# Batch 1's first half as the second chunk, its attention in float32 products, and the check for the general path inside the last feed forward

## Chip, cores and metric

The kernel runs on one core of a Trainium2 chip. The metric is the device time of one execution in microseconds (us), the median of three runs.

## What is computed

Sliding-window attention with a few always visible first keys ("sinks"), followed by a feed forward with a squared ReLU. Everything is float32; 4 batches, 8 heads of 64, 768 positions, model width 512, inner width 2048.

```python
B, H, S, D = 4, 8, 768, 64          # n_sink = 4, window = 128
scores = matmul(q, k.T) / sqrt(D)
keep = (pos[None, :] < n_sink) | ((rel >= 0) & (rel < window))
a = softmax(where(keep, scores, -1e9))
x = matmul(a, v)                     # heads side by side: (B*S, 512)
h = x @ w_in                         # (3072, 2048)
r = maximum(h, 0.0)
g = s * (r * r) + b
out = g @ w_out                      # (3072, 512)
```

## The kernel before

The 3072 tokens are cut into 8 chunks of 384: chunk `c` is half `c % 2` of batch `c // 2`. A first half needs only its own 384 keys; a second half also the block ahead of it and the sinks.

Chunk 0's attention stands alone at the start (`first_slots`), in plain float32 products: a score product `fa` (a float32 product is recorded as two matmuls), a masked minimum on VectorE (L445), an exponential on ScalarE (L449), the division by the row's sum on VectorE (`fn`, L457 to L460), the transpose `fb` (L468, copied out by L472), and the product with v, `fc` (L480), whose result each head copies out by itself into the pair's half of `k.x` (L482, L483). A head is three units of 128 rows.

All later chunks use `attn_slots`: each operand is split into a high part and a rest in a reduced format that TensorE takes as one product (the dtype fp32r of the rows), so that a product is two or three cheaper ones. The splitting is done by ScalarE, VectorE and GpSimd (`prep_head`, L268 to L278; the transposed weights L321 and L322), the sinks of a second half go through a product of their own (L305, L367 to L382).

The feed forward of a chunk is `moe_steps`: for each of 16 blocks `f` of the inner width, `l1(f)` makes 12 matmuls (L521), then L524, L525, L527 and L528 make the two parts of `g`; `l2(f)`, two steps later, makes 9 matmuls (L539). That is 32 steps. While the feed forward of chunk c runs, the slots of the attention of chunk c+1 are dealt out between its steps.

During chunk 0's attention and its feed forward the weights are made from the raw 64-bit words (`make_weight`): per block two ScalarE passes (L198, L199), two VectorE passes (L200, L201), a GpSimd addition (L203), a ScalarE copy (L208) and a subtraction (L214) on VectorE or, for each fourth block, GpSimd. From the second feed forward on they stay in memory.

The order of instructions on each engine is set by a scheduler when the program is built, from the order of the code and from when buffers come free; on the chip each engine takes its instructions in that order. All loads and stores are issued from SyncE's queue (SP).

At the end `bad` collects whether the inputs are outside what this path handles (more sinks or a wider window than laid out for, or a row with nothing to keep); a product `cnt` sums it up, `flag` is loaded into a register of each engine by `values_load`, and `tc.If(go > 0)` runs the general path, which these inputs do not need. The last chunk's three output tiles `ot` use the two buffers of the tag `hl`.

Of the kernel before, what the change touches and what calls it, by code (L numbers as in the profile page):

```python
# [15 lines left out]
P = 128  # L16
B, H, S, D = 4, 8, 768, 64
NS = 16
# [15 lines left out]
E0, LB0, LC0 = 8, 4, 6  # L34
LB, LC, LD, L2 = 2, 4, 1, 2
# [3 lines left out]
def tile_kernel(ctx, tc, qT, kT, k0, v, vsk, n_sink, window, w, s, b, out):  # L39
# [15 lines left out]
    m_all = first.tile([P, 6 * P], MDT, tag="m", name="m_all")  # L55
# [34 lines left out]
    nc.sync.dma_start(lim[:, 0, :], n_sink.partition_broadcast(P))  # L90
    nc.sync.dma_start(lim[:, 1, :], window.partition_broadcast(P))
# [324 lines left out]
    def first_slots():  # L416
        k = Chunk()

        q = [wk.tile([P, NCC, CH], F32, tag=f"x{i}", name=f"q0{i}") for i in range(2)]
        k.x = [wk.tile([P, NCC, CH], F32R, tag=f"x{i}", name=f"x{i}_0") for i in range(2)]  # L420
        kk = first.tile([P, NCC, CH], F32, tag="k0", name="k0")
        vv = first.tile([P, NCC, CH], F32, tag="v0", name="v0")
        cc, tt, zz, sms = {}, {}, {}, {}

        def load():
            nc.gpsimd.memset(q[0][D:], 0.0)
            nc.vector.memset(q[1][:D], 0.0)
            for ps_ in (slice(0, 1), slice(1, NCC)):
                for hh in range(2):
                    hs = slice(hh * D, (hh + 1) * D)  # L430
                    nc.sync.dma_start(q[hh][hs, ps_, :], qT[0, ps_, hs, :CH].rearrange("r e s -> e r s"))
                    if hh == 0:
                        nc.sync.dma_start(kk[:, ps_, :], k0[:, ps_, :])
                nc.sync.dma_start(vv[:, ps_, :].rearrange("p r (n e) -> p r n e", n=BLK),
                                  v[0, ps_, :, :BLK].rearrange("r p n h d -> p r n (h d)"))

        def fa(h, i):
            pr = h // 2
            n = (i + 1) * P
            u = h * BLK + i  # L440
            uu = slice(u, u + 1)
            sc = psO.tile([P, 512], F32, tag="po", name="sc0")
            nc.tensor.matmul(sc[:, :n], q[h % 2][:, pr, i * P:(i + 1) * P], kk[:, pr, :n], start=True, stop=True)
            sm = first.tile([P, CH], F32, name="sm0", tag="sm0", bufs=E0)
            nc.vector.tensor_tensor_reduce(out=sm[:, :n], in0=sc[:, :n], in1=m_full[i], scale=-0.125, scalar=BIG,  # L445
                                           op0=ALU.add, op1=ALU.min, accum_out=negm[:, uu])
            if i == 0:
                zz[h] = first.tile([P, 2, BLK], F32, name="z0", tag="z0", bufs=4)
# [296 lines left out]
```

## Time and profile before

| | us |
|---|---|
| median of 3 runs (from 781.71 to 782.03) | 781.77 |
| the profiled execution, its own time | 781.77 |
| its span, first to last instruction | 780.0 |
| of it TensorE busy | 735.3 |
| VectorE, ScalarE, GpSimd busy | 513.6, 495.5, 268.8 |

The profile is one execution. "Busy" of an engine is the time in which at least one of its instructions was under way; an average over the span hides that the stages have different limits, so that busy times are read by stage below. The profiled execution's own time is that of the median, so that a difference in the span can be set against the median directly.

### The profile page before, as it was taken

Reading aid. Unit: us, or ns where it says so; the run is one execution under the profiler, and the core shown is the slowest. Engines: PE = TensorE matmul, PEld = TensorE weight load, DVE = VectorE, ACT = ScalarE, POOL = GpSimd, SP = SyncE. Lnnn points to the kernel's source line nnn. Section 1 sums busy time; section 2 is a strip of 40 time slices with the busy share of each in tenths; the row PEclk is TensorE's granted clock in tenths of the full one; section 3 lists DMA queues with packets and bytes.
Section 4 is the critical chain, followed back from the end, with each engine's and each line's share of the span. In section 5 each row is a group of like instructions: output and inputs, shape, how many; then the busy total and the mean of one; then the engine's idle time right before and its main releaser. Section 6 shows DMA issues by size and latency. Waiting matters only on the chain.

```text
span 780.0 us, 12112 instructions
## 1 busy us (share of the span) xinstructions
PE 735.3 (94%) x4036; PEld 656.9 (84%) x4036; DVE 513.6 (66%) x1250; ACT 495.5 (64%) x1231; POOL 268.8 (34%) x411
## 2 busy tenths in 40 slices
PE   7977988699999999999999999999999999999996
PEld 4655776579999999899999999899989999899985
DVE  6879998985676467655676466665676466663231
ACT  4886977766666576656666576656666576643222
POOL 3057668652343233322243233332343233210000
PEclk9989999999999999999999999999999999999998
DMA  7636205212112212112112212112111212001001
GB/s 271 273 103 229 105 14 170 76 34 77 42 54 59 73 43 67 35 43 76 43 53 57 76 43 62 40 43 76 43 53 55 77 43 60 21 1 42 1 1 45
DMA packets 28118, 54.21 MB, mean 70 GB/s; under 512 B 3600, under 2 KB 16528, under 8 KB 26128
## 3 DMA queue, kind: packets, MB, share of 16 engines
q1 hardware_dynamic: 28048, 53.36, 21.3%
q8 instruction: 34, 0.56, 0.3%
q14 instruction: 36, 0.29, 0.1%
HBM read 47.06 MB, written 6.29 MB: 68 GB/s over the span
## 4 chain that ended last, share of the span: by engine, by line
PE 76%; DVE 8%; ACT 7%; issue 3%; POOL 3%; DMA 2%; SPq 1%; ACTq 0%; POOLq 0%; DVEq 0%
PE h L521 30%; PE po L539 30%; PE o L354 5%; PE sc L294 2%; PE sc L293 2%; PE tp L317 2%; PE tp L316 2%; ACT w L199 1%; DVE r L525 1%; DMA w<-in_w 1%; PE o L480 1%; POOL w L203 1%; DVE w L201 1%; DVE qs L272 1%; ACT sm L304 1%
## 5 line engine op out<-in xcount | busy, mean ns | idle before, releaser
L521 PE MATMUL h<-x,w 128*128 128x384 f32 x1536 | 299.5, 343 | 8.7 <-DVE hl L322 3.8
L539 PE MATMUL po<-w,g 128*128 128x512 f32 x1152 | 301.6, 403 | 5.7 <-ACT g L527 3.7
L521 PEld LDWEIGHTS h<-x,w 128*128 128x128 f32 x1536 | 269.7, 190 | 14.5 <-issue 4.0
L539 PEld LDWEIGHTS po<-w,g 128*128 128x128 f32 x1152 | 211.6, 191 | 47.7 <-ACT g L527 4.9
L524 ACT ACTIVATE r<-h 128x384 f32<-128x384 f32 x128 | 62.9, 491 | 103.9 <-PE h L521 96.9
L298 DVE CUSTOM_DVE_ANT_0 sm<-sc,msk 128x272 f32<-128x272 f32 (+1 forms) x168 | 70.2, 418 | 78.4 <-PE sc L294 55.9
L525 DVE SCALAR_TENSOR_TENSOR r<-r,sb 128x384 f32<-128x384 f32 x128 | 84.1, 657 | 54.1 <-ACT r L524 54.0
L528 DVE SCALAR_TENSOR_TENSOR g<-r,sb,g 128x384 fp32r<-128x384 f32 x128 | 85.5, 668 | 45.6 <-ACT g L527 43.5
L305 POOL COPY psk<-sm 128x48 f32<-128x48 f32 x168 | 52.2, 311 | 162.9 <-ACT sm L304 161.7
L304 ACT ACTIVATE sm<-sm,negm 128x272 f32<-128x272 f32 (+1 forms) x168 | 85.4, 508 | 23.3 <-DVE negm L298 22.3
L527 ACT ACTIVATE g<-r,sb 128x384 fp32r<-128x384 f32 x128 | 78.7, 614 | 33.2 <-DVE r L525 32.1
L273 POOL TENSOR_TENSOR kl<-kraw,kh 128x544 fp32r<-128x544 f32 (+1 forms) x56 | 74.9, 1337 | 56.8 <-ACT kh L271 55.5
L321 ACT CAST hl<-tp 128x256 fp32r<-128x256 f32 (+1 forms) x168 | 58.8, 352 | 26.4 <-PE tp L317 26.2
L354 PE MATMUL o<-hl,vv 128*128 128x256 f32 (+1 forms) x400 | 71.4, 295 | 1.1 <-DVE hl L322 0.8
L322 DVE TENSOR_TENSOR hl<-tp,hl 128x256 fp32r<-128x256 f32 (+1 forms) x168 | 66.8, 398 | 7.5 <-ACT hl L321 6.7
L278 POOL TENSOR_TENSOR vv<-vraw,vv 128x256 fp32r<-128x256 f32 (+1 forms) x56 | 41.9, 747 | 60.9 <-ACT vv L277 59.0
L354 PEld LDWEIGHTS o<-hl,vv 128*128 128x128 f32 x400 | 54.9, 190 | 2.7 <-DVE hl L322 1.1
L293 PE MATMUL sc<-kh,qs 128*128 128x272 f32 (+1 forms) x168 | 47.8, 284 | 5.8 <-DVE hl L322 4.7
L363 DVE TENSOR_TENSOR xm<-o,y 64x384 f32<-64x384 f32 x56 | 31.0, 553 | 31.5 <-ACT y L362 31.3
L294 PE MATMUL sc<-kl,qs 128*128 128x272 f32 (+1 forms) x168 | 48.5, 289 | 0.0
L203 POOL TENSOR_TENSOR w<-w 128x1024 int32<-128x1024 int32 (+1 forms) x17 | 32.6, 1921 | 42.4 <-DVE z L458 19.3
L317 PE MATMUL tp<-identr,sm 128*128 128x128 f32 x168 | 45.7, 272 | 0.0
(112 smaller groups left out, 852.0 us busy)
## 6 DMA issues: line engine op xcount, KB each, us to landing
w<-in_w SPq DMA_DIRECT2D x15, 1024.0 KB, 8.9
kraw<-in_kT SPq DMA_DIRECT2D x32, 272.0 KB, 2.7
out<-ot SPq DMA_DIRECT2D x24, 256.0 KB, 2.0
qraw<-in_qT SPq DMA_DIRECT2D x28, 192.0 KB, 2.4
kraw<-in_kT SPq DMA_DIRECT2D x24, 208.0 KB, 2.4
vraw<-in_v SPq DMA_DIRECT2D x16, 256.0 KB, 2.7
vraw<-in_v SPq DMA_DIRECT2D x12, 192.0 KB, 2.3
vsraw<-in_vsk SPq DMA_DIRECT2D x28, 64.0 KB, 1.8
```

The source lines that it names most:

```text
L273: nc.gpsimd.tensor_tensor(out=hd.kl[:, :kw], in0=hd.k[:, :kw], in1=hd.kh[:, :kw].bitcast(F32), op=ALU.subtract)
L293: nc.tensor.matmul(sc[:, :n], hd.qs[:, qs], hd.kh[:, c0:c0 + n], start=True, stop=False)
L294: nc.tensor.matmul(sc[:, :n], hd.qs[:, qs], hd.kl[:, c0:c0 + n], start=False, stop=True)
L298: nc.vector.tensor_tensor_reduce(out=sm[:, :n], in0=sc[:, :n], in1=m, scale=-0.125, scalar=BIG, op0=ALU.add, op1=ALU.min, accum_out=negm[: ...
L304: nc.scalar.activation(sm[:, :n], sm[:, :n], AF.Exp, bias=negm[:, uu], scale=-1.0, accum_out=pp.zz[:, i, hh:hh + 1])
L322: nc.vector.tensor_tensor(out=lo, in0=tp[:, a:z], in1=hi.bitcast(F32), op=ALU.subtract)
L354: nc.tensor.matmul(hd.o[:, q0:q0 + n * P], hd.vv[:, kb, :], hd.hl[:, t, c0 * P:(c0 + n) * P], start=(hd.n == 0), stop=(i == BLK - 1 and kb ...
L521: nc.tensor.matmul(h[:, :CH], weight[f][:, 0, wi, cc * P:(cc + 1) * P], x[xi][:, cc, :], start=(i == 0), stop=(i == 11))
L525: nc.vector.scalar_tensor_tensor(out=r, in0=r, scalar=s_ap, in1=r, op0=ALU.mult, op1=ALU.mult)
L527: nc.scalar.activation(gg[:, 0, :], r, AF.Identity, bias=b_ap, scale=1.0)
L528: nc.vector.scalar_tensor_tensor(out=gg[:, 1, :], in0=r, scalar=b_ap, in1=gg[:, 0, :].bitcast(F32), op0=ALU.add, op1=ALU.subtract)
L539: nc.tensor.matmul(po[tb], gg[:, gi, tsl], weight[f][:, 1, wi, :], start=(f == 0 and i == 0), stop=(f == NF - 1 and i == 2))
```

## The change

1. The chunks are worked in the order 0, 2, 1, 3, 4, 5, 6, 7 (`ORDER`). Chunk 2, the first half of batch 1, is now the one whose attention runs beside chunk 0's feed forward, and it is computed by `plain_slots`, the former `first_slots` made to serve both chunks: float32 products, no splitting. Its zero-padded q and v come in per pair of heads (`load_pair`), its tiles share tags with the split path.
2. In `plain_slots`, for both chunks, v is laid out per head with zeros in the other head's 64 columns, so that both heads of a pair add up in one bank of the accumulation memory. One copy (L525) and one subtraction (L526) of 128 partitions per pair take the place of two each of 64 partitions. For v there are 8 loads in chunk 0 instead of 2, in runs of 256 bytes instead of 1536.
3. `out_of_range`, the check, stands after the ninth step of the last feed forward instead of behind everything.
4. The limits and the first pair's v are loaded from ScalarE's queue, the masks `m_all` live on in another pool, and the last chunk's third output tile uses the tag `ot`.

```diff
+ORDER = 0, 2, 1, 3, 4, 5, 6, 7
...
-    nc.sync.dma_start(lim[:, 0, :], n_sink.partition_broadcast(P))
-    nc.sync.dma_start(lim[:, 1, :], window.partition_broadcast(P))
+    nc.scalar.dma_start(lim[:, 0, :], n_sink.partition_broadcast(P))
+    nc.scalar.dma_start(lim[:, 1, :], window.partition_broadcast(P))
...
+                for pr in range(rs.start, rs.stop):
+                    for hh in range(2):
+                        hs = slice(hh * D, (hh + 1) * D)
+                        (nc.scalar if pr == 0 else nc.sync).dma_start(v0[:, pr, :, hh, hs], v[0, pr, :, :BLK, hh, :])
...
+        def load_pair(pr):
+            kt = wk.tile([P, 544], F32, tag="kh", name="k_p")
+            nc.sync.dma_start(kt[:, :CH], k0[bb, :, pr, :])
+            for hh in range(2):
+                h = 2 * pr + hh
+                own, other = halves(h)
+                kk[h] = kt
+                q[h] = wk.tile([P, CH], F32, tag="qs", name="q_p")
+                nc.gpsimd.memset(q[h][other], 0.0)
+                nc.sync.dma_start(q[h][own], qT[bb, pr, own, :CH])
+                vv[h] = wk.tile([P, 4, P], F32, tag="vv", name="v_p", bufs=VB)
+                nc.gpsimd.memset(vv[h][:, :BLK, other], 0.0)
+                nc.sync.dma_start(vv[h][:, :BLK, own], v[bb, pr, :, :BLK, hh, :])
...
         def fc(h):
-            pr, hs = h // 2, slice(h % 2 * D, (h % 2 + 1) * D)
-            o = ps("o0")
+            pr, hh = h // 2, h % 2
+            if hh == 0:
+                os_[pr] = ps("o0")
+            o = os_[pr]
...
-                nc.tensor.matmul(o[:, kb * P:CH], vv[:, pr, kb * P:(kb + 1) * P], t[:, c0:c0 + (BLK - kb) * P],
-                                 start=(kb == 0), stop=(kb == BLK - 1))
-            nc.scalar.copy(k.x[0][hs, pr, :], o[hs, :CH])
-            nc.vector.tensor_tensor(out=k.x[1][hs, pr, :], in0=o[hs, :CH], in1=k.x[0][hs, pr, :].bitcast(F32), op=ALU.subtract)
+                nc.tensor.matmul(o[:, kb * P:CH], vv[h][:, kb, :], t[:, c0:c0 + (BLK - kb) * P],
+                                 start=(hh == 0 and kb == 0), stop=(hh == 1 and kb == BLK - 1))
+            if hh == 1:
+                nc.scalar.copy(k.x[0][:, pr, :], o[:, :CH])
+                nc.vector.tensor_tensor(out=k.x[1][:, pr, :], in0=o[:, :CH], in1=k.x[0][:, pr, :].bitcast(F32), op=ALU.subtract)
...
+        lb, lc = (LB0, LC0) if c == 0 else (3, 5)
...
-    for c in range(NC_):
-        steps = moe_steps(k.x, store_at(c), wk, before if c == 0 else None, c == NC_ - 1)
+    for j, c in enumerate(ORDER):
+        steps = moe_steps(k.x, store_at(c), wk, before if j == 0 else None, j == NC_ - 1)
...
-            k, slots = attn_slots(c + 1)
+            k, slots = (plain_slots if j == 0 else attn_slots)(ORDER[j + 1])
...
+            if j == NC_ - 1 and n == NF // 2:
+                go = out_of_range()
```

VectorE in the middle of chunk 0's feed forward, before: `hl`, `xm`, `xsk`, `qs` and `sm` belong to the split attention of chunk 1, `wt` and `w` to the weights, `r` and `g` to the feed forward.

```order
L322 TENSOR_TENSOR hl<-tp,hl 128x256 x2
L363 TENSOR_TENSOR xm<-o,y 64x384
L370 TENSOR_TENSOR xsk<-ts,xsk 32x384
L298 ISA sm,negm<-sc,msk 128x272
L298 ISA negm 128x1
L381 TENSOR_TENSOR xm<-os,xm 128x384
L382 TENSOR_TENSOR xm<-zb,xm 128x384
L200 TENSOR_SCALAR wt<-w_714 128x1024
L525 SCALAR_TENSOR_TENSOR r<-r,sb 128x384
L201 SCALAR_TENSOR_TENSOR w_714<-w_714,wt 128x1024
L528 SCALAR_TENSOR_TENSOR g<-r,sb,g 128x384
L272 TENSOR_TENSOR qs<-qraw,qs 64x384
```

VectorE at the like place now: `sm_p` and `z_p` are the weights and sums of chunk 2's plain attention, `x_2` its result.

```order
L202 SCALAR_TENSOR_TENSOR w_752<-w_752,wt 128x1024
L576 SCALAR_TENSOR_TENSOR g<-r,sb,g 128x384
L494 TENSOR_SCALAR z_p<-z_p 128x3
L201 TENSOR_SCALAR wt<-w_814 128x1024
L495 RECIPROCAL z_p<-z_p 128x3
L202 SCALAR_TENSOR_TENSOR w_814<-w_814,wt 128x1024
L497 TENSOR_SCALAR sm_p<-sm_p,z_p 128x128
L497 TENSOR_SCALAR sm_p<-sm_p,z_p 128x256
L497 TENSOR_SCALAR sm_p_837<-sm_p_837,z_p 128x384
L526 TENSOR_TENSOR x_2_524<-o_801,x_2_523 128x384
L215 TENSOR_TENSOR w_936<-w_689,w_936 128x2x512
```

The splits and the sinks' sums are gone from between the weight passes (the line numbers are those of the changed file); the divisions L497, three in a row per head, are new there.

ScalarE in chunk 0's attention, before, where it comes to the first weights `w_257` (`tt` are copied transposes, `sm` exponentials, three of each to a head):

```order
L472 COPY tt_179<-tp_203 128x3x128
L449 ACTIVATE sm_210,z_201<-sm_210,negm 128x256
L198 ACTIVATE w_257<-w_257 128x1024
L472 COPY tt_213<-tp_214 128x128
L449 ACTIVATE sm_219,z_201<-sm_219,negm 128x384
L472 COPY tt_213<-tp_227 128x2x128
L482 CAST x_0_104<-o_231 64x384
```

ScalarE now, where it comes to the first weights `w_263`:

```order
L512 COPY tt_221<-tp_249 128x3x128
L512 COPY tt_259<-tp_260 128x128
L512 COPY tt_259<-tp_281 128x2x128
L512 COPY tt_259<-tp_296 128x3x128
L199 ACTIVATE w_263<-w_263 128x1024
L487 ACTIVATE sm_303,z_294<-sm_303,negm 128x256
L525 CAST x_0_106<-o_239 128x384
```

The first weight pass stood behind 8 exponentials and 3 copies; it stands behind 13 and 9 now.

SP's last rows, before (`out` are the stores, `flag` the check's result):

```order
L250 DMA kraw<-in_kT 128x544 x2
L237 DMA vraw<-in_v 128x512
L636 DMA out<-ot 128x512 x5
L697 TENSOR_LOAD flag
L697 ISA x2
L636 DMA out<-ot 128x512
L698 COMPARE_AND_BRANCH
```

and now:

```order
L251 DMA kraw<-in_kT 128x544 x2
L238 DMA vraw<-in_v 128x512
L684 DMA out<-ot 128x512 x3
L719 TENSOR_LOAD flag
L719 ISA x2
L684 DMA out<-ot 128x512 x3
L751 COMPARE_AND_BRANCH
```

The load of the flag stood ahead of the last store; now it stands ahead of the last chunk's three.

## Rows read from the trace of the kernel before

**Rows 1.** The page: span, busy time by engine, granted clock in 40 slices.

```profile
span 780.0 us, 12112 instructions
...
PE 735.3 (94%) x4036; PEld 656.9 (84%) x4036; DVE 513.6 (66%) x1250; ACT 495.5 (64%) x1231; POOL 268.8 (34%) x411
...
PEclk9989999999999999999999999999999999999998
```

**Rows 2.** Busy time in stretches: length, then each engine's, clock, DMA share, GB/s.

```profile
0.00:49.40 49.40, 38.51 (x158) 24.97 (x159) 35.38 (x131) 35.37 (x94) 12.51 (x28) 0.91 0.58 216
49.40:177.60 128.20, 104.20 (x519) 86.81 (x519) 119.34 (x196) 99.88 (x201) 86.02 (x76) 0.94 0.33 112
177.60:264.05 86.45, 85.97 (x494) 79.22 (x493) 55.60 (x148) 55.86 (x152) 27.99 (x53) 1.00 0.19 55
264.05:353.45 89.40, 89.07 (x517) 82.29 (x517) 57.57 (x148) 58.33 (x152) 29.70 (x53) 1.00 0.18 55
...
705.10:780.00 74.90, 67.53 (x339) 60.67 (x337) 19.95 (x33) 20.27 (x37) 0.74 (x1) 0.96 0.07 23
```

**Rows 3.** The chain of waits from 49.4 to 177.6, shares by line.

```profile
by line: issue 13.2%; ACT w L199 7.3%; PE po L539 7.3%; POOL w L203 6.4%; DVE r L525 6.0%; DVE qs L272 5.8%; DVE w L201 5.1%; DVE wt L200 4.6%; DMA kraw<-in_kT 3.9%; DVE w L214 3.8%; DVE g L528 3.5%; ACT w L198 3.4%; ACT sm L304 3.1%; POOL 
```

**Rows 4.** VectorE by line, 49.4 to 177.6: busy us, mean ns, idle before.

```profile
L528 DVE SCALAR_TENSOR_TENSOR g<-r,sb,g 128x384 fp32r<-128x384 f32 x16 | 16.0, 997 | 1.1 <-ACT g L527 1.1
...
L272 DVE TENSOR_TENSOR qs<-qraw,qs 64x384 fp32r<-64x384 f32 x9 | 12.1, 1343 | 0.3
```

**Rows 5.** VectorE by line, 0 to 49.4, the same columns.

```profile
L460 DVE TENSOR_SCALAR sm<-sm,z 128x128 f32<-128x128 f32 (+2 forms) x24 | 9.4, 447 | 0.1
L445 DVE CUSTOM_DVE_ANT_0 sm<-sc,m_all 128x128 f32<-128x128 f32 (+2 forms) x24 | 9.3, 417 | 1.6 <-PE sc L443 1.5
L483 DVE TENSOR_TENSOR x<-o,x 64x384 fp32r<-64x384 f32 x7 | 3.9, 551 | 0.1
...
L445 DVE DVE_READ_ACCUMULATOR2_ANT negm<- 128x1 f32 x24 | 2.0, 81 | 0.0
...
L458 DVE RECIPROCAL z<-z 128x3 f32<-128x3 f32 x8 | 1.4, 172 | 0.1
...
L457 DVE TENSOR_SCALAR z<-z 128x3 f32<-128x3 f32 x8 | 1.3, 162 | 4.0 <-ACT sm L449 4.0
```

**Rows 6.** The timeline of chunk 0's attention: start, us, engine, instruction, idle before.

```profile
10.41 0.88 DVE L460 TENSOR_SCALAR sm<-sm,z 128x128 f32<-128x128 f32 x3
...
16.70 1.10 ACT L198 ACTIVATE w<-w 128x1024 int32<-128x1024 uint32 x1 [2.94 <-DMA w<-in_w]
...
27.15 1.46 PE L480 MATMUL o<-tt,v 128*128 128x384 f32 x6
...
28.45 0.49 PE L468 MATMUL tp<-identr,sm 128*128 128x128 f32 x3
...
28.78 1.47 PE L443 MATMUL sc<-k,q 128*128 128x128 f32 x6
...
29.20 1.90 POOL L203 TENSOR_TENSOR w<-w 128x1024 int32<-128x1024 int32 x1 [19.27 <-DVE z L458]
...
29.42 2.35 DVE L460 TENSOR_SCALAR sm<-sm,z 128x128 f32<-128x128 f32 x3
...
43.06 0.61 PE L468 MATMUL tp<-identr,sm 128*128 128x128 f32 x3 [3.52 <-DVE sm L460]
```

**Rows 7.** The loads from 4.9 to 8: packets, MB, share of 16 engines.

```profile
q1 hardware_dynamic: 473, 0.76, 94.8%
```

**Rows 8.** The loads from 46.5 to 50, the 64 KB of `vsraw`.

```profile
q1 hardware_dynamic: 144, 0.07, 6.4%
```

**Rows 9.** The timeline of the last 10 us.

```profile
771.17 1.29 ACT L543 ACTIVATE ot<-po 128x512 f32<-128x512 f32 x2 [3.03 <-PE po L539]
...
772.67 0.15 DVE L694 CAST flag<-cnt 1x1 int32<-1x1 f32 x1 [3.88 <-PE cnt L692]
773.92 0.60 ACT L543 ACTIVATE ot<-po 128x512 f32<-128x512 f32 x1 [1.46 <-DMA out<-ot]
```

More of the change, by code (lines that the diff above doesn't have):

```diff
@@ L413, in attn_slots, with plain_slots, halves, load_all @@
         return k, [slot(t) for t in range(n + LC + LD)]
-    def first_slots():
+    def plain_slots(c):
         k = Chunk()
[L419 to L428, printed above, removed]
+        k.c, bb = c, c // 2
+        q, kk, vv, cc, tt, zz, os_ = {}, {}, {}, {}, {}, {}, {}
+        if c == 0:
+            q0 = [wk.tile([P, NCC, CH], F32, tag=f"x{i}", name=f"q0{i}") for i in range(2)]
+            k0_ = first.tile([P, NCC, CH], F32, tag="k0", name="k0")
+            v0 = first.tile([P, NCC, BLK, 2, P], F32, tag="v0", name="v0")
+            for h in range(H):
+                q[h] = q0[h % 2][:, h // 2, :]
+                kk[h] = k0_[:, h // 2, :]
+                vv[h] = v0[:, h // 2, :, h % 2, :]
+        k.x = [wk.tile([P, NCC, CH], F32R, tag=f"x{i}", name=f"x{i}_{c}") for i in range(2)]
+        def halves(h):
+            own, other = slice(0, D), slice(D, P)
+            return (own, other) if h % 2 == 0 else (other, own)
+        def load_all():
+            nc.gpsimd.memset(q0[0][D:], 0.0)
+            nc.vector.memset(q0[1][:D], 0.0)
+            for rs in (slice(0, 1), slice(1, NCC)):
@@ L500, in f @@
                         fn(t // BLK, i)
-                if 0 <= t - LB0 < n:
-                    fb(*units[t - LB0])
-                if 0 <= t - LC0 < n and (t - LC0) % BLK == BLK - 1:
-                    fc((t - LC0) // BLK)
+                if 0 <= t - lb < n:
+                    fb(*units[t - lb])
+                if 0 <= t - lc < n and (t - lc) % BLK == BLK - 1:
+                    fc((t - lc) // BLK)
             return f
-        return k, [slot(t) for t in range(n + LC0)]
+        return k, [slot(t) for t in range(n + lc)]
     def moe_steps(x, store, wk, before=None, last=False):
@@ L541, in l2 @@
                 if f == NF - 1:
-                    ot = wk.tile([P, DM], F32, name="ot", **(dict(tag="hl", bufs=HLB) if last else dict(tag="ot")))
+                    ot = wk.tile([P, DM], F32, name="ot", **(dict(tag="hl", bufs=HLB) if last and tb < 2 else dict(tag="ot")))
                     nc.scalar.mul(ot, po[tb], 1.0 / WUP)
@@ L655, in before, with out_of_range @@
         weights(f + 2 + LOADS // 2, 2 * f + 5)
+    def out_of_range():
+        bad = const.tile([P, 4], F32, tag="bad", name="bad")
+        nc.vector.tensor_reduce(out=bad[:, 0:1], in_=negm, axis=AX.X, op=ALU.max)
+        nc.vector.tensor_scalar(out=bad[:, 0:1], in0=bad[:, 0:1], scalar1=0.9e9, scalar2=None, op0=ALU.is_ge)
+        tc.keep_in_program_order(nc.vector.tensor_scalar(out=bad[:, 1:2], in0=n_ap, scalar1=float(NS), scalar2=None, op0=ALU.is_gt))
+        nc.vector.tensor_scalar(out=bad[:, 2:3], in0=w_ap, scalar1=float(P), scalar2=None, op0=ALU.is_gt)
+        nc.vector.tensor_scalar(out=bad[:, 3:4], in0=w_ap, scalar1=1.0, scalar2=None, op0=ALU.is_lt)
+        bad1 = const.tile([P, 1], F32, tag="bad1", name="bad1")
+        nc.vector.tensor_reduce(out=bad1, in_=bad, axis=AX.X, op=ALU.max)
+        cnt = ps("cnt")
+        nc.tensor.matmul(cnt[0:1, 0:1], bad1, one, start=True, stop=True)
+        flag = const.tile([1, 1], I32, tag="flag", name="flag")
+        nc.vector.tensor_copy(flag, cnt[0:1, 0:1])
+        go = nc.values_load(flag, min_val=0, max_val=P)
+        return go
     NC_ = 2 * B
-    k, slots = first_slots()
+    k, slots = plain_slots(0)
     for i, f in enumerate(slots):
```

72 lines of the change are left out of this document (36 added, 36 removed).

## The prediction

> **What bounds the kernel now.** The page comes first. TensorE is busy for 735.3 of 780.0 us, VectorE and ScalarE for about two thirds [rows 1]; that would make TensorE the limit everywhere. The granted clock says otherwise for the start: it is at its full level of 2.4 GHz except in the first quarter, where slices show means of 8 and 9 tenths, part of the time at the lower level of 1.2 GHz, and at the very end [rows 1]. So I cut the span into stages, at the first L521 of each chunk, and read the engines by stage [rows 2]. From 177.6 on, a stage is as long as TensorE is busy: 85.97 of 86.45 us where the feed forward has a first half's attention beside it, 89.07 of 89.40 where it has a second half's. VectorE and ScalarE stand at 55 to 58 there. In the stage from 49.4 to 177.6, chunk 0's feed forward with chunk 1's attention and the making of the weights, the same work of TensorE takes 128.20 us; VectorE is busy for 119.34 of them, 93%, and the clock is 0.94. The chain of waits of this stage jumps among weight passes on ScalarE, VectorE and GpSimd, and VectorE's L525, L272 and L528 [rows 3]; TensorE's own lines are a small part. This stage is bound by VectorE and by queues that hold each other up, and it is 128.20 - 89.40 = 38.8 us longer than its TensorE work needs. The stage ahead of it, chunk 0's attention, has no full engine either (38.51, 35.38 and 35.37 of 49.40 us).
>
> So work that is taken from VectorE is worth time in the first 178 us only, and work that is added to TensorE costs its full time after 178 us, and before that as much as TensorE's slack doesn't hold.
>
> **Stage of the first feed forward: what is removed.** The split attention of a second half costs VectorE 57.57 - 19.95 = 37.6 us where it is undisturbed (a late stage less the last one, which has the feed forward alone) [rows 2]. Here it costs more: L272 takes 1343 ns each, 9 times [rows 4], while the subtraction of the same shape L483 takes 551 ns [rows 5]; that is 9 x 0.79 = 7.1 us of blocking on top, 44.7 together. ScalarE loses 58.33 - 20.27 = 38.1 us and GpSimd 29.70 - 0.74 = 29.0 us [rows 2].
>
> **What is added.** Plain attention on VectorE, from chunk 0's: 9.4 + 9.3 + 2.0 + 1.4 + 1.3 us, and four subtractions of 0.55 = 2.2 in place of eight, together 25.6 us [rows 5]. VectorE in this stage then comes to 119.3 - 44.7 + 25.6 = 100.2 us. On TensorE, back to back, a head takes 1.47 us for its three scores, 1.46 for its product with v, and 2 x 0.49 for six transposes [rows 6]: 3.91 us, 31.3 for eight heads. The split form costs 89.07 - 67.53 = 21.5 [rows 2]. So TensorE needs 67.5 + 31.3 = 98.8 us here, 9.8 more than now. Two engines thus ask for 99 and 100 us each, and the slack of TensorE, 38.8 us now, falls to about ten.
>
> **The stage's new length.** By VectorE alone and its present share of 93% it would be 100.2 / 0.931 = 107.6 us. I add 4: waits of TensorE that now vanish in its slack will no longer all do so, and the weights end before the stage does, so that its last fifth is TensorE's alone while the part ahead of it is VectorE's. I take 112, that is 16.2 us less than 128.2. The bounds: 103 if the two interleave nearly without loss (TensorE's 98.8 and 4%), 120 if the blocking below comes in full.
>
> **The blocking.** Three divisions L460 in a row take 0.88 us at 10.41, where GpSimd is idle, and 2.35 at 29.42, just behind the start of a GpSimd addition L203 at 29.20 [rows 6]; an L272 here and the L528 with its 997 ns [rows 4] are lengthened in the same way. Eight such triples now stand among GpSimd's weight additions. Against that GpSimd loses 29 of its 86 us, so that what is left on VectorE, L525 and L528 above all, is blocked less often. I set the two against each other at nothing; if all eight triples took 2.35 us it would be 8 x 1.47 = 11.8 us more on VectorE, and (100.2 + 11.8) / 0.931 = 120.3, in the sum below 773 us. The Trainium skill ("SBUF — State Buffer", section "Who interferes with whom") speaks against the change here: VectorE and GpSimd share a pair of ports that is locked for a whole instruction, tensor_scalar in its fast mode (the divisions) among those that take it, and the later one waits. The two rows agree with it; the removed L272, two inputs from SBUF against a reading GpSimd, is in that rule as well.
>
> **Queues that the change lengthens.** GpSimd now clears the unused half of the next q and v, and such a clear waits until TensorE is through with the buffer; behind it in GpSimd's queue stand weight additions, in SP's the loads of q hold weight loads back in the same way. I count nothing: in the new order the addition behind such a clear serves a product about two feed forward blocks on, each block 4.2 us of TensorE (67.5 / 16), against 1.90 us for an addition [rows 6]. Without that cover it would be up to 2 us for each of eight heads, in the range of the 120 above.
>
> **The other stages.** Chunk 1's attention now runs where chunk 2's did, in a stage that TensorE bounds: 89.40 instead of 86.45, a loss of 2.95 us [rows 2]. The others keep theirs.
>
> **Chunk 0's attention.** Four copies and four subtractions fewer, 1.9 and 2.2 us. ScalarE stood 2.94 us for the first weights at 16.70 [rows 6], with copies and exponentials behind; now 14 more of them are ahead of that pass, about 6 us of work. Against this, v comes in 3072 runs of 256 bytes where it came in 512 of 1536. A packet of 1.5 KB takes 0.948 x 16 x 3.1 / 473 = 0.099 us of one of 16 engines [rows 7], one of 512 bytes 0.064 x 16 x 3.5 / 144 = 0.025 us [rows 8]; so v took 3.2 us of all engines and will take between 2.4 (by bytes) and 4.8 (by packets). The first weights come up to 3 us later, with six SP issues for v instead of two; the 6 us cover that. I take 2 us off, between a loss of 1 and a gain of 4.9 (all of 2.94 and of the copies). The two queues to which issues moved have nothing urgent: ScalarE's first exponential waits for the masks.
>
> **The end.** The third output copy began at 773.92, 1.46 us after the second ended, for want of a buffer [rows 9]; it will begin at once. Its store no longer stands behind the load of the flag, which was there at 772.82. I take 1.5 us off, between 1 and 2. The check's few small VectorE operations and one product of a column fall where VectorE is busy for 19.95 of 74.90 us; TensorE pays some 0.2 us.
>
> **The sum**, against the profiled execution's own 781.77 us, which is also the median: -16.2 + 2.95 - 2.0 - 1.5 = -16.8, so **765.0 us**.
>
> **Rivals.**
> - *The ports stay the limit.* Stage of 117 to 124 us, time from 770 to 777. For it: 2.35 against 0.88 us, and 1343 ns for L272. Against it: GpSimd has a third less to do. 0.15.
> - *The stage runs close to TensorE's need.* 102 to 106 us and all of the 4.9 in chunk 0's attention: 752 to 759. For it: ScalarE gets back less than the 38.1 us that it loses (the whole first stretch has 35.37 us of it, weights included), so that all three are near 100 or below, and a busier TensorE is granted more of its clock (0.94 now). Against it: two engines at nearly the same load never run without loss in queues that are in order. 0.20.
> - *Not faster: each head's transposes wait for its divisions.* Scores, masked minimum, exponential, sums of all three units, divisions, transposes are a chain that the split form lacks up to the transposes; at 43.06 TensorE waited 3.52 us for it [rows 6]. With that wait for each head the stage is 98.8 + 8 x 3.52 = 127.0, and the time 780; from 3.75 us per head (a stage of 128.8) it is slower than before. Against it: the stage has feed forward products between, and the order puts some of them between a head's last score and its first transpose. 0.05.
> - *The product's price is the lower clock.* At 0.8, the lowest slice of the page [rows 1], TensorE's 98.8 us become 123.5, and with the 4 us of the forecast for waits the stage is 127.5: no change, or a little slower. For that the clock would have to fall as it did in chunk 0's attention, where TensorE idled; here it has work. 0.03.
>
> **Chances and range.** The forecast, a stage of 107 to 116 us and so 760 to 769, has 0.57. The time is the stage's length plus 653. The range leaves out most of the two rivals at 780 and the tails of the others: 755 to 774, with about 0.82 inside. Below 0.2% (1.6 us), a difference counts as none, which is about what a measurement of this kernel can tell: the first three cases are faster, and the 0.08 at 780 are divided into 0.01 faster, 0.03 the same and 0.04 slower: faster 0.93, same 0.03, slower 0.04.
>
> **What the changed profile would show.** The second stage from about 47 to 159; VectorE near 100 us in it and TensorE above 85% busy at a clock over 0.94; three divisions at 0.9 us or at over 2, which decides about the ports; no wait of ScalarE for the first weights over 1 us; the stage with chunk 1's attention at 89.4 us; the last output copy right behind the second, and 1.5 us less from TensorE's last product to the end. The prediction is wrong if TensorE's waits for L497 add up to over 10 us, if the stage's length follows GpSimd's additions, or if weights come late at the start.

## The result, and the profile after

| | kernel before | changed kernel |
|---|---|---|
| time, median of 4 | 781.74 us (781.64 to 782.03) | 775.68 us (775.54 to 776.47) |
| ratio, 95% interval | | 0.9926 [0.9912, 0.9939] |
| span of the profiled execution | 780.0 us | 773.9 us |

The change gains 6.1 us, where 16.8 were forecast; 775.7 lies outside the range of 755 to 774. The page of the changed kernel answers to [rows 1]: less work on VectorE and ScalarE, the same on TensorE, and a clock that is below 9 tenths in the fifth slice, some 77 to 97 us, and at the very end.

```profile
span 773.9 us, 11988 instructions
...
PE 733.9 (95%) x4024; PEld 654.0 (85%) x4024; DVE 496.9 (64%) x1222; ACT 477.9 (62%) x1187; POOL 237.0 (31%) x377
...
PEclk9999899999999999999999999999999999999998
```

The same by stages, columns as in [rows 2]: first the second stage, here from the first product L569 (L521 before) at 42.09 us to the first one of the next chunk at 169.51; then the stage with chunk 1's attention; then the last feed forward.

```profile
42.09:169.51 127.42, 105.27 (x489) 84.81 (x488) 103.65 (x173) 83.80 (x166) 51.94 (x38) 0.95 0.27 93
169.67:259.03 89.36, 89.05 (x518) 82.23 (x517) 57.60 (x148) 58.07 (x151) 29.80 (x52) 1.00 0.21 61
700.10:773.90 73.80, 67.58 (x338) 60.48 (x336) 19.95 (x33) 20.15 (x37) 0.61 (x1) 0.97 0.06 23
```

Against [rows 2], the first two stages together end at 169.5 in place of 177.5: -7.9, where -18.2 was forecast. The stage of chunk 1's attention is 89.36 in place of 86.45, +2.9 (forecast +2.95). The last is 73.80 in place of 74.90, -1.1 (forecast -1.5). The sum is -6.1, and nearly the whole miss, 10.3 of 10.7 us, lies in the first two stages. Taken by itself the second stage did not get shorter: it is 127.42 us long, where it was 127.99 from 49.46 to 177.45 and 112 was forecast. It only begins 7.4 us sooner. VectorE's work in it, 103.65 us, is near the 100.2 of the forecast; but it is busy for 81% of the stage, not 93%, and TensorE for 83%.

Two stretches of 60 us within this stage show how VectorE's work lies in time:

```profile
50.00:110.00 60.00, 45.94 (x201) 36.16 (x202) 59.82 (x86) 41.28 (x73) 29.89 (x19) 0.91 0.33 118
110.00:170.00 60.00, 52.95 (x256) 43.59 (x255) 38.86 (x81) 35.08 (x82) 20.12 (x20) 0.97 0.18 57
```

From 50 to 110 us VectorE is full and TensorE idles for 14 us, at a mean clock of 0.91, part of the time at the 1.2 GHz level; from 110 on VectorE is at 65%. VectorE by line from 42 to 170 us (busy us, mean ns) shows what fills it:

```profile
L573 DVE SCALAR_TENSOR_TENSOR r<-r,sb 128x384 f32<-128x384 f32 x16 | 19.9, 1243 | 4.5 <-ACT r L572 4.5
...
L497 DVE TENSOR_SCALAR sm_p<-sm_p,z_p 128x128 f32<-128x128 f32 (+2 forms) x24 | 12.5, 576 | 0.1
...
L494 DVE TENSOR_SCALAR z_p<-z_p 128x3 f32<-128x3 f32 x8 | 5.5, 690 | 0.5 <-ACT sm_p L487 0.5
```

The timeline of the changed kernel shows why these are long. The small addition L494, 3 elements wide, takes 0.17 us alone and 1.85 us beside a GpSimd addition L204, and ends within 0.02 us of it (89.98 + 1.85 = 91.83; 89.61 + 2.20 = 91.81). Three divisions take 0.88 or 2.54 us. So it goes for three of the eight additions L494 (1.85, 1.86 and 1.00 us) and three of the eight triples of divisions (2.53, 2.54 and 3.06 us, the last beside a GpSimd subtraction L215); the others stay at 0.15 to 0.17 and 0.87 to 0.88 us.

```profile
89.61 2.20 POOL L204 TENSOR_TENSOR w<-w 128x1024 int32<-128x1024 int32 x1 [1.17 <-DVE w L202]
89.98 1.85 DVE L494 TENSOR_SCALAR z_p<-z_p 128x3 f32<-128x3 f32 x1
...
93.76 2.54 DVE L497 TENSOR_SCALAR sm_p<-sm_p,z_p 128x128 f32<-128x128 f32 x3
93.92 1.89 POOL L204 TENSOR_TENSOR w<-w 128x1024 int32<-128x1024 int32 x1 [1.89 <-DVE w L202]
...
118.74 0.17 DVE L494 TENSOR_SCALAR z_p<-z_p 128x3 f32<-128x3 f32 x1 [0.47 <-ACT sm_p L487]
...
119.16 0.88 DVE L497 TENSOR_SCALAR sm_p<-sm_p,z_p 128x128 f32<-128x128 f32 x3
```

What TensorE waits for in this stage (us in total, times, longest):

```profile
PE tp L509 <- DVE sm_p L497: 10.0, 6, 2.5
PE h L569 <- ACT w L209: 3.3, 1, 3.3
PE po L587 <- DVE g L576: 2.6, 2, 2.0
```

The transposes wait 10.0 us for the divisions, right at the bound over which the forecast called itself wrong. At the end of the kernel all three output copies stand in one row of the timeline, where the third began 1.46 us after the second [rows 9]:

```profile
766.34 1.98 ACT L591 ACTIVATE ot<-po 128x512 f32<-128x512 f32 x3 [3.02 <-PE po L587]
```

### The profile page after: what moved, and what is told of

It reads as the page before. It is cut to its first block, busy times and chain, and to the rows that moved or that the text cites. A ratio compares the mean times of both kernels' runs of the same rounds, so it can differ in the third digit from the quotient of the medians.

```text
span 773.9 us, 11988 instructions
## 1 busy us (share of the span) xinstructions
PE 733.9 (95%) x4024; PEld 654.0 (85%) x4024; DVE 496.9 (64%) x1222; ACT 477.9 (62%) x1187; POOL 237.0 (31%) x377
## 4 chain that ended last, share of the span: by engine, by line
PE 78%; DVE 9%; ACT 3%; issue 2%; POOL 1%; DMA 1%; ACTq 0%; DVEq 0%; POOLq 0%
PE h L569 32%; PE po L587 30%; PE o L355 5%; PE sc L295 2%; PE sc L294 2%; PE tp L318 2%; DVE w L202 2%; PE tp L317 2%; DVE r L573 1%; DVE w L215 1%; DVE wt L201 1%; DVE sm_p L497 1%; PE o L522 1%; DVE g L576 1%; PE ts L368 1%
## 5 line engine op out<-in xcount | busy, mean ns | idle before, releaser
L569 PE MATMUL h<-x,w 128*128 128x384 f32 x1536 | 299.7, 344 | 3.6 <-ACT w L209 3.3
L569 PEld LDWEIGHTS h<-x,w 128*128 128x128 f32 x1536 | 270.5, 190 | 7.5 <-ACT w L209 3.7
L573 DVE SCALAR_TENSOR_TENSOR r<-r,sb 128x384 f32<-128x384 f32 x128 | 88.7, 693 | 55.2 <-ACT r L572 55.2
L299 DVE CUSTOM_DVE_ANT_0 sm<-sc,msk 128x272 f32<-128x272 f32 (+1 forms) x144 | 60.8, 422 | 80.4 <-PE sc L295 65.5
L306 POOL COPY psk<-sm 128x48 f32<-128x48 f32 x144 | 38.3, 266 | 166.0 <-ACT sm L305 164.7
L305 ACT ACTIVATE sm<-sm,negm 128x272 f32<-128x272 f32 (+1 forms) x144 | 73.7, 512 | 20.4 <-DVE negm L299 19.1
L274 POOL TENSOR_TENSOR kl<-kraw,kh 128x544 fp32r<-128x544 f32 (+1 forms) x48 | 61.3, 1278 | 56.3 <-ACT kh L272 50.0
L322 ACT CAST hl<-tp 128x256 fp32r<-128x256 f32 (+1 forms) x144 | 51.3, 356 | 28.7 <-PE tp L318 28.2
L323 DVE TENSOR_TENSOR hl<-tp,hl 128x256 fp32r<-128x256 f32 (+1 forms) x144 | 57.9, 402 | 8.1 <-ACT hl L322 7.3
L355 PE MATMUL o<-hl,vv 128*128 128x256 f32 (+1 forms) x352 | 61.5, 293 | 0.0
L279 POOL TENSOR_TENSOR vv<-vraw,vv 128x256 fp32r<-128x256 f32 (+1 forms) x48 | 34.7, 724 | 59.8 <-ACT vv L278 57.4
L204 POOL TENSOR_TENSOR w<-w 128x1024 int32<-128x1024 int32 (+1 forms) x17 | 33.0, 1946 | 53.8 <-DVE w L202 28.2
L295 PE MATMUL sc<-kl,qs 128*128 128x272 f32 (+1 forms) x144 | 41.4, 287 | 0.0
L294 PE MATMUL sc<-kh,qs 128*128 128x272 f32 (+1 forms) x144 | 40.4, 280 | 0.0
```

The source lines that it names most:

```text
L274: nc.gpsimd.tensor_tensor(out=hd.kl[:, :kw], in0=hd.k[:, :kw], in1=hd.kh[:, :kw].bitcast(F32), op=ALU.subtract)
L295: nc.tensor.matmul(sc[:, :n], hd.qs[:, qs], hd.kl[:, c0:c0 + n], start=False, stop=True)
L305: nc.scalar.activation(sm[:, :n], sm[:, :n], AF.Exp, bias=negm[:, uu], scale=-1.0, accum_out=pp.zz[:, i, hh:hh + 1])
L323: nc.vector.tensor_tensor(out=lo, in0=tp[:, a:z], in1=hi.bitcast(F32), op=ALU.subtract)
L355: nc.tensor.matmul(hd.o[:, q0:q0 + n * P], hd.vv[:, kb, :], hd.hl[:, t, c0 * P:(c0 + n) * P], start=(hd.n == 0), stop=(i == BLK - 1 and kb ...
L569: nc.tensor.matmul(h[:, :CH], weight[f][:, 0, wi, cc * P:(cc + 1) * P], x[xi][:, cc, :], start=(i == 0), stop=(i == 11))
```

## The experiments

Three theories. **A**: VectorE is full, and lengthened, because GpSimd's weight additions block it. **B**: the chain that makes a weight (ScalarE, VectorE, GpSimd, ScalarE, VectorE) is what TensorE waits for. **C**: each head's chain from scores to transposes is. Every edit also lets the scheduler place neighbouring instructions a little otherwise. Line numbers shift with the edits; the names of the tiles don't. "Wide" weights are those made in one piece of 128x1024, 13 of the 16 blocks; the six additions for the narrow halves of the last three stay in every run. e4, e5, e14 and e19 leave the lowest three bits out of the wide weights, to learn what the additions cost. Runs beside one another had the kernel before at 781.5 to 782.1 us (medians); ratios are to it. "Stage end" is the start of the first product of the second feed forward in the profiled execution (before 177.45, changed 169.51). That execution isn't always the median: e2's and e3's took 2.8 and 2.7 us more than theirs, e11's 2.1 more, e6's and e7's 1.8 and 1.5 less.

| run | median us | ratio, 95% interval | stage end |
|---|---|---|---|
| e1 L573 from the bank | 774.1 | 0.9898 [0.9872, 0.9925] | 167.24 |
| e2 divisions on ScalarE | 767.1 | 0.9805 [0.9775, 0.9834] | 163.33 |
| e3 first half as before | 777.8 | 0.9948 [0.9934, 0.9962] | 173.96 |
| e4 no GpSimd addition | 757.0 | 0.9672 [0.9642, 0.9702] | 150.53 |
| e5 addition off the chain | 774.3 | 0.9905 [0.9883, 0.9928] | 167.35 |
| e6 bits on VectorE | 762.0 | 0.9746 [0.9728, 0.9764] | 154.05 |
| e7 = e6 and e2 | 759.1 | 0.9706 [0.9689, 0.9722] | 151.28 |
| e9 = e2 and dummies | 773.7 | 0.9897 [0.9871, 0.9923] | 167.62 |
| e10 before, bits on VectorE | 773.7 | 0.9899 [0.9883, 0.9916] | 168.46 |
| e11 = e7 and e1 | 762.5 | 0.9744 [0.9717, 0.9770] | 157.68 |
| e12 attention later | 781.5 | 1.0000 [0.9988, 1.0011] | 175.00 |
| e13 = e11 and e12 | 762.1 | 0.9755 [0.9738, 0.9771] | 155.27 |
| e14 before, no addition | 768.4 | 0.9839 [0.9812, 0.9866] | 163.74 |
| e15 longer distance | 771.8 | 0.9875 [0.9855, 0.9896] | 165.31 |
| e16 = e7 and e15 | 754.2 | 0.9644 [0.9624, 0.9663] | 148.76 |
| e17 = e7, L215 on VectorE | 754.0 | 0.9646 [0.9627, 0.9665] | 147.22 |
| e18 = e16 and e17 | 751.2 | 0.9614 [0.9597, 0.9631] | 143.77 |
| e19 = e4 and e15 | 750.8 | 0.9602 [0.9586, 0.9618] | 144.77 |

### What GpSimd's additions cost: e4, e5

The comments in the cuts of code name the run that each line is from.

```diff
-                nc.gpsimd.tensor_tensor(out=hi, in0=hi, in1=lo, op=ALU.add)
+                if len(raws[f]) > 1:                                             # e4
+                    nc.gpsimd.tensor_tensor(out=hi, in0=hi, in1=lo, op=ALU.add)  # e4
+                nc.gpsimd.tensor_tensor(out=hi if len(raws[f]) > 1 else lo, in0=hi, in1=lo, op=ALU.add)  # e5
```

> The changed kernel without GpSimd's 13 additions L204 of the wide weights: the lowest three bits that they add to each weight are left out, and nothing else. It bounds what blocking by these additions and their place in the weights' chain cost together. Theory A (blocking): VectorE's L573, L576 and divisions return to about 0.65, 0.65 and 0.3 us, VectorE loses 15 to 20 us in the stage, and the time falls by 8 to 14 us, to 762 to 768. Theory B (chain of the weights): each weight is made 2 us sooner, and the time falls by 3 to 8 us. Theory C (the chain of each head): 2 to 4 us less.

> The changed kernel with GpSimd's additions L204 of the wide weights kept, of the same size and at the same place, but written into the dead low words: no later pass of the weights waits for them, and the lowest three bits stay out of the weights, as in the run without these additions (756.96 us). The two together tell blocking from chain. Theory A (the additions cost because they lengthen VectorE's instructions): VectorE's L573 stays over 1 us, and the time stays at 772 to 777. Theory B (they cost because each stands in the chain that makes a weight): the time falls nearly as in that run, to 757 to 762. Between: both.

Without the wide additions 757.0 us, 18.7 less than the changed kernel and more than any theory had; with the additions kept at the same place, but off the weights' chain, 774.3. So by these two runs some 1.4 of the 18.7 us are the chain (B), and some 17 are what the additions do to others (A); in these 17 is also what they hold up in GpSimd's own queue, which no run tells apart. The second stage of e4, then that of e5:

```profile
39.88:150.53 110.65, 99.42 (x490) 81.98 (x488) 88.61 (x174) 84.96 (x169) 25.35 (x27) 0.98 0.31 107
```

```profile
40.37:167.35 126.98, 105.57 (x489) 85.55 (x488) 102.79 (x174) 86.43 (x168) 49.09 (x38) 0.93 0.27 94
```

VectorE does the same work in both (174 instructions), in 88.6 and in 102.8 us. In e4 the divisions are back at 0.86 to 0.88 us for three. The feed forward's squaring (L574 there, L573 in the changed kernel) is not always short: it takes 0.62 us at its median, but 2.57 to 2.77 us in the three places where GpSimd makes a wide subtraction L216 (L215 in the changed kernel). These block as the additions do. TensorE, too, does the same in 99.4 and in 105.6 us, at a mean clock of 0.98 and of 0.93; it idles for 11 and for 21 us.

### The kernel before without them: e14, and bits on VectorE: e6, e10

e14 is e4's edit on the kernel before. e6 brings the low bits of the wide weights in on VectorE, without GpSimd (ScalarE rounds them down, so that no carry is needed, and the lowest bit can differ); e10 is e6's edit on the kernel before:

```diff
-                nc.scalar.activation(lo, lo.bitcast(U32), AF.Copy, scale=2.0 ** -29)
+                nc.scalar.activation(lo, lo.bitcast(U32), AF.Copy, scale=0.996 * 2.0 ** -29, bias=-0.484)
...
-                nc.vector.tensor_scalar(out=t, in0=hi, scalar1=3, scalar2=None, op0=ALU.logical_shift_left)
+                nc.vector.scalar_tensor_tensor(out=t, in0=hi, scalar=3, in1=lo,
+                                               op0=ALU.logical_shift_left, op1=ALU.bitwise_or)
```

> The kernel before without GpSimd's additions of the wide weights (their lowest three bits are left out), the partner of the changed kernel without them, 756.96 us. If blocking by these additions is all that kept the change from its forecast, this run is at 771 to 776, 14 to 19 us above its partner. If a part of the miss has another cause (each head's chain), the distance is 8 to 13 us: 765 to 770.

> The changed kernel with the low bits brought in on VectorE: L201 takes (high word shifted by 3) or (low bits) as one instruction with two SBUF inputs, ScalarE rounds the low bits down so that no carry is needed, and GpSimd's 13 additions for wide weights go. Against the run without additions (756.96) VectorE pays about 1.22 in place of 0.68 us, twice for each of 13 wide weights' passes at most: 7 to 14 us of VectorE, of which the part up to 110 us counts. Theory A (blocking) and theory B (chain) both: 758 to 766. If GpSimd's additions had cost nothing but order: 775 to 783.

> The kernel before (without the change) with the edit that brought the changed kernel to 761.98 us: low bits on VectorE, no GpSimd additions for wide weights. It says what the change is worth when this blocking is gone. If blocking is all that kept the change from the 16.8 us forecast, this kernel is at 775 to 780, since VectorE at 93% with second-half attention stays its limit, and the change is then worth 13 to 18 us. If blocking cost the kernel before as much, it is at 764 to 769, and the change is worth about 6 us with or without it: then VectorE's mere load is the error, not the ports.

The kernel before gains 13.4 us (781.8 to 768.4), the changed one 18.7. So the change is worth 768.4 - 757.0 = 11.4 us without these additions and 6.1 with them. By e6 and e10 it is worth 773.7 - 762.0 = 11.7. e10 fell between the two outcomes laid down for it; e14 came in the second of its own, in which a part of the miss has another cause. The additions make 5 to 6 us of the missing 10.7, and not all of it. The second stage of e14:

```profile
44.99:163.74 118.75, 99.94 (x519) 85.18 (x518) 109.89 (x196) 98.59 (x202) 63.49 (x66) 0.96 0.35 121
```

In this stage alone the additions cost the changed kernel 127.42 - 110.65 = 16.8 us and the kernel before 127.99 - 118.75 = 9.2; ahead of it they cost the kernel before more (4.5 us against 2.2), so that 5.3 remain.

### VectorE relieved: e1, e2, e9

```diff
-            nc.vector.scalar_tensor_tensor(out=r, in0=r, scalar=s_ap, in1=r, op0=ALU.mult, op1=ALU.mult)
+            nc.vector.scalar_tensor_tensor(out=r, in0=h[:, :CH], scalar=su_ap, in1=r, op0=ALU.mult, op1=ALU.mult)   # e1
...
+            if c:
+                nc.scalar.activation(sm[:, :n], sm[:, :n], AF.Identity, scale=z[:, 0, i:i + 1])   # e2, e9
...
+                nc.vector.tensor_scalar(out=zero, in0=zero, scalar1=z[:, 0, i:i + 1], scalar2=None, op0=ALU.mult)   # e9
```

> The changed kernel with one edit: L573 takes the product h from its PSUM bank (scaled by s / 256) as one factor in place of r from SBUF, so that it has one SBUF input where it had two. Theory A (VectorE is full from 48 to 110 us because GpSimd's weight additions lengthen its instructions with two SBUF inputs): L573 falls from 1243 to about 650 ns in the first feed forward, 16 x 0.6 = 9.5 us off VectorE, of which the 10 blocks up to 110 us count; the time falls by 3 to 6 us, to 770 to 773. Theory B (the stage waits for the chain that makes the weights and for loads held up in SP's queue): within 1 us of 775.7. Theory C (each head's scores, exponential, divisions and transposes are the chain): 0 to 1.5 us less.

> The changed kernel with the 24 divisions of the plain attention beside the first feed forward on ScalarE in place of VectorE. They took 12.5 us of VectorE there, 576 ns each. Theory A (VectorE full and lengthened): VectorE about 91 us in the stage, the time falls by 3 to 7 us, to 769 to 773; ScalarE grows from 84 to about 92 us. Theory B (weight chain): within 1.5 us of 775.7, or slower, since ScalarE's weight passes now queue behind the divisions. Theory C (the chain of each head): TensorE's waits of 10.0 us for the divisions fall by half at least and the time by 3 to 5 us, whatever VectorE does.

> The 24 divisions on ScalarE as in the earlier run (767.12 us), and on VectorE 24 multiplications of the same form and sizes, at the same places, on a tile of zeros that nobody waits for: VectorE's load is that of the changed kernel, the transposes don't wait for VectorE. Theory A (VectorE's load counts): back to 773 to 777. Theory C (the chain of each head counts): stays at 766 to 770.

e1 made L573 (here L574) as short as expected, 611 ns, but its neighbours grew: the divisions from 576 to 715 ns, the weight pass L202 (here L203) from 1138 to 1267. VectorE's total fell by 5.0 us (98.63 against 103.65), not 10.1, and the time by 1.5 to 2.2, below the 3 to 6 of theory A. About half of what L573 lost of blocking came back on what VectorE had next.

```profile
L203 DVE SCALAR_TENSOR_TENSOR w<-w,wt 128x1024 int32<-128x1024 int32 (+1 forms) x15 | 18.9, 1267 | 0.0
...
L498 DVE TENSOR_SCALAR sm_p<-sm_p,z_p 128x128 f32<-128x128 f32 (+2 forms) x24 | 15.9, 715 | 0.1
...
L574 DVE SCALAR_TENSOR_TENSOR r<-h,su,r 128x384 f32<-128x384 f32 x16 | 9.8, 611 | 4.2 <-ACT r L573 4.2
```

e2 gained 8.6 us, more than any theory had. e9, with the load put back on VectorE but off the transposes' way, lost 6.6 of it again (773.7). So most of it was VectorE's load. But the waits of TensorE in e9 show that C isn't out: the transposes now wait 10.8 us for ScalarE's divisions, which need the sums L494 and L495 from the full VectorE.

```profile
PE tp L514 <- ACT sm_p L498: 10.8, 7, 3.5
```

### Chunk 0's attention: e3

```diff
-    k, slots = plain_slots(0)
+    k, slots = first_slots()
```

> The changed kernel, but chunk 0's attention ahead of the first feed forward in the form of the kernel before: v loaded in runs of 1536 bytes, each head a bank and an evacuation of its own; chunk 2's plain attention as in the changed kernel. If the new form of chunk 0 gains the 2 us that the forecast gave it, this run is 2 us slower, 777 to 778.5. If it lost instead, since v's loads now take the queue until 13.4 us and the first weights are issued 6.6 us later (14.41 in place of 7.80), this run is 1 to 4 us faster, 772 to 774.5.

777.8 us, 2.1 more than the changed kernel by medians, 1.7 by the ratios, whose intervals just overlap: the new form of chunk 0 gains about what was forecast for it. In the profiles e3's second stage begins at 49.58 us, as in the kernel before (49.46), and the changed kernel's at 42.09; but e3's is 3.0 us shorter (124.38 against 127.42), and by the medians only some 2 of the 7.5 us reach the end.

### Attention spread otherwise: e12, e15, e19

```diff
-            while i < len(slots) and i * len(steps) < (n + 1) * len(slots):
+            wait = 4 if j == 0 else 0                                                                # e12
+            while i < len(slots) and i * (len(steps) - wait) < (n + 1 - wait) * len(slots):          # e12
...
-        lb, lc = (LB0, LC0) if c == 0 else (3, 5)
+        lb, lc = (LB0, LC0) if c == 0 else (5, 7)                                                    # e15, e19
```

e15 and e19 also issue both loads of q of a pair ahead of its loads of v; e19 has e4's edit besides.

> The changed kernel with chunk 2's attention beginning four steps of the first feed forward later (29 slots over the last 14 steps of 18 in place of all 18). VectorE was full from 50 to 110 us and at 65% from 110 to 170. Theory A (VectorE's load and its place in time): moving some 6 us of attention out of the full stretch gives 3 to 7 us, 769 to 773. Theory that each head's chain or the end of the weights bounds the stage: the same or slower, 775 to 782, since the attention ends no sooner and has less time.

> The changed kernel with the transposes of a unit of chunk 2 five units behind its scores in place of three, the products with v seven in place of five; the two loads of q of a pair ahead of its two loads of v, so that the later release of v's buffers doesn't hold q back. Theory C (each head's chain makes TensorE wait 10.0 us for the divisions): these waits fall to 3 us or less and the time by 3 to 7 us, 769 to 773. Theory A (VectorE is full, whatever stands behind it): other waits take their place, 774 to 777.

> The changed kernel without GpSimd's additions of the wide weights (lowest three bits left out) and with the longer distance between a unit's scores and its transposes. If the two causes add, 757.0 - 4 = 753 us, 15 us below the kernel before without additions (768.4), and the account of the 16.8 us is closed within 2 us. If the chain's waits were themselves made by the blocked VectorE, the distance gives nothing here: 756 to 758.

e12 was to move 6 us of VectorE's work out of the full stretch, and by theory A to gain; the time rose to that of the kernel before. It moved less than meant: from 50 to 110 us VectorE is still busy for 57.2 us, in place of 59.8. The same attention in fewer steps puts fewer feed forward products between a head's scores and its transposes, which now wait 16.0 us:

```profile
PE tp L509 <- DVE sm_p L497: 16.0, 7, 3.6
```

The clock of this stage fell to 0.88 with it. e15, the opposite, makes 3.9 us: the waits of the transposes for the divisions fell from 10.0 to 0.8 us (the last line), others of 3 us each have come:

```profile
PE tp L512 <- DVE negm L484: 3.9, 3, 3.0
PE h L572 <- ACT w L209: 3.3, 1, 3.3
PE h L572 <- DVE w L215: 3.1, 1, 3.1
...
PE tp L512 <- DVE sm_p L500: 0.8, 1, 0.8
```

Without the additions the distance gives 6.1 us (e19 against e4), so that the two make more together than one by one. Both causes gone, the second stage is

```profile
39.95:144.77 104.82, 98.26 (x490) 81.50 (x489) 89.16 (x174) 83.53 (x169) 28.08 (x27) 1.00 0.32 113
```

TensorE needs 98.26 us at a clock of 1.00, where the forecast had 98.8. e19 ends this stage at 144.77 and e14, the kernel before without additions, at 163.74: -19.0, against -18.2 forecast and -7.9 measured. In time, 768.37 - 750.84 = 17.5 us. e14 has no longer distance of its own, so that this is not the change alone.

### A faster kernel: e7, e11, e13, e16, e17, e18

e7 joins e6 and e2; e11 adds e1 to it, e13 e12 to that; e16 is e7 with e15's distance; e17 is e7 with all of L215 on VectorE; e18 joins e16 and e17.

```diff
-                e = nc.gpsimd if f % 4 == 3 else nc.vector
+                e = nc.vector
```

> Two edits together: the low bits on VectorE without GpSimd's additions, and the 24 divisions on ScalarE. If VectorE's load and lengthening is what the stage stands on, the two add in part: 752 to 760. TensorE's need of the stage, 98.8 us, sets the floor at about 749. If the divisions' gain of some 9 us was only blocking by GpSimd that is now gone, it equals the run with the low bits on VectorE within 2 us.

> Three edits on the changed kernel: low bits on VectorE, divisions on ScalarE, L573 reading h from its bank. 759.11 us was measured without the last. If blocking by what GpSimd still does (three L215 and six narrow additions) lengthens L573 from 0.62 to 0.73 us only, the gain is 21 x 0.1 = 2 us of VectorE at most: 756 to 759.

> The three edits of the run before last and the later start of chunk 2's attention together. If VectorE's full stretch is still the limit there (it is at 95 to 100% from 50 to 90 us), 753 to 757; if with the lighter VectorE TensorE is near its need up to 120 us, then the later attention only crowds the end: 758 to 764.

> The fastest kernel so far (low bits on VectorE, divisions on ScalarE, 759.11 us) with the same longer distance. There VectorE is no longer full all the time, and TensorE waits 3.8 us for exponentials of the heads: theory C 754 to 757, theory A 758 to 760.

> The fastest kernel so far (759.11 us) with the last three wide subtractions L215 taken from GpSimd to VectorE: 8.1 us of GpSimd go, VectorE pays 3 x 1.2 us. Theory A (blocking costs as long as GpSimd reads beside a full VectorE): 754 to 758. If VectorE's load alone counts: 760 to 763.

> All that helped together, the whole computation: low bits on VectorE, divisions on ScalarE, the longer distance, the last three wide subtractions on VectorE. 754.2 and 754.0 us were measured with one of the last two each, 759.1 with neither: 749 to 753 if they add, with TensorE's need of the stage at about 749 as the floor.

e7 came to 759.1, at the slow end of its forecast. e11 is 3.4 us slower, not faster: reading h from its bank, which then stays occupied longer, doesn't pay when little blocks L573; that the bank is the reason wasn't shown. In the profiles e11's stage ends 6.4 us later than e7's, and 4.1 of these lie ahead of the stage (43.38 against 39.30 us). e13 is like e11. e16 gains 4.9 us and e17 5.1 us on e7: five subtractions more on VectorE (three wide, two of the narrow weights), 11 us less of work on GpSimd, and a faster kernel. e18 takes 751.2 us, 24.4 less than the changed kernel and 30.4 less than the kernel before as run beside it (781.6). Its second stage, with TensorE at 95%, is as long as TensorE needs and 5 us:

```profile
39.74:143.77 104.03, 98.86 (x489) 82.74 (x488) 85.98 (x155) 91.57 (x191) 15.44 (x22) 0.98 0.33 117
```

## Why the prediction was wrong

**The amounts of work** were nearly right: VectorE 103.65 us for 100.2, TensorE 98.26 at full clock (e19) for 98.8. What failed is how the forecast made a length of them, by two steps.

**The blocking** is the step that failed first: "I set the two against each other at nothing". It reckoned that GpSimd loses 29 of its 86 us. But what it loses is the work of the split attention, while the additions of 1.9 us and more stay, and stand, from 50 to 110 us, beside a VectorE that is full: many an instruction that comes next is held. They cost the changed kernel 18.7 us and the kernel before 13.4: the missing term is 5.3 us in the time, and 16.8 - 9.2, some 7.5 us, in the stage. The Trainium skill ("SBUF — State Buffer", section "Who interferes with whom") has the lock last for the whole instruction of the other engine; the trace agrees (L494's 1.85 us for 3 elements, ended with L204's 2.20). The forecast named this rule, had the rival that rests on it at 770 to 777 with a chance of 0.15, and the time fell there. Its stage did not: 127.42 us, longer than the 117 to 124 of that rival, and a start that made up for it. (The forecast's own figure for all eight triples, 120.3, makes 773.3 in its sum, not below 773.)

**The length of the stage** is the other: "100.2 / 0.931 = 107.6 us. I add 4", together 112, where 127.42 was measured. The 4 us for waits of TensorE stood for the transposes' 10.0 us as well, which the rival of that name put aside because "the stage has feed forward products between". The order had the transposes three units behind their scores, too near beside a full VectorE: e15 gives back 3.9 us, and 6.1 without the additions. Taking over the 93% was wrong too: VectorE is at 100% for 60 us and at 65% for the next 60. To start the attention later (e12) lost time, but hardly spread the load, so that what an even load would be worth stays open.

**The account**: of the first two stages' gain, 7.9 us with both causes in, 13.2 without the additions (e4 against e14: 163.74 - 150.53), 19.0 without either; 18.2 was forecast. Where these lie is another matter (us in the profiled executions):

| | stage begins | its length | its end |
|---|---|---|---|
| kernel before | 49.46 | 127.99 | 177.45 |
| forecast | about 47 | 112 | 159 |
| changed kernel | 42.09 | 127.42 | 169.51 |
| before, no addition (e14) | 44.99 | 118.75 | 163.74 |
| changed, no addition (e4) | 39.88 | 110.65 | 150.53 |
| e4 with the distance (e19) | 39.95 | 104.82 | 144.77 |

The 19.0 are 5.0 ahead of the stage and 13.9 in it, the 18.2 were 2.0 and 16.2; and e19's stage is as long as TensorE needs and 6.6 us, while the forecast had VectorE set its length. That the two totals are near each other is in part luck.

**The clock.** The forecast took TensorE's work at its price at full clock, and a rival let a busier TensorE be granted more; the mean went from 0.94 to 0.95 only. TensorE's 98.3 us of work took 105.27 in the changed kernel: some 7 us more, of which a mean of 0.95 makes about 5 (98.26 / 0.95 = 103.4, an estimate). In e19, with 6.6 us of idle time in place of 22, the clock is 1.00. Over the 20 profiles the mean of this stage is 0.88 to 0.97 where TensorE idles for 15 us or more, and 0.96 to 1.00 where it idles for less. So a wait of TensorE tends to cost more than its own length; how much more was not measured.

**Queues that the change lengthens** were counted at nothing. No run tells this apart by itself: e15 changes the order of the loads and the distance together. In the changed kernel GpSimd's additions waited 28.2 us in all for VectorE, and the clears of v 15.6 us for TensorE, with additions queued behind them; what the second cost stays open. SyncE's loads of q and v waited 40.6 and 45.0 us for TensorE; in the kernel before, its loads of keys waited 66.7 us for GpSimd.

**The other steps held**, one of them by luck. Chunk 1's attention +2.9 for +2.95. Chunk 0's attention -1.7 to -2.1 (e3) for -2.0, with no wait for the first weights; but its end came 7.4 us sooner, beyond the 4.9 that the forecast allowed, with TensorE busy there for 32.6 us (153 products recorded) at a clock of 1.00 in place of 38.6 (158) at 0.91, which the sum did not have; and by e3 most of those 7.4 us don't reach the end. The end -1.1 for -1.5. Of the signs named ahead, VectorE near 100 us, the stage of 89.4 and the last copy came; the second stage to 159 and TensorE above 85% didn't, and the divisions came both at 0.9 us and at over 2.

## What to carry to other kernels

Where VectorE is full, GpSimd work beside it isn't free help: ask what the kernel loses with it left out, and try it on VectorE itself (e6, e17: more work on VectorE, 5 to 14 us faster). Shortening a blocked instruction hands part of the block to the next ones (e1: about half). When a change takes work off one engine, look at how far apart the new work's producer and its reader stand in order, before dividing loads by a share of busy time.

## What was not expected of the hardware

Blocking doesn't go by the size of the blocked instruction: 3 elements took 1.85 us in place of 0.17. The first feed forward product began between 42.09 (changed kernel) and 46.50 us (e1), though the products ahead of it stand in the same order in both; why was not shown.
